# A fused attention, expert and feed-forward kernel: the attention loop goes by two head pairs at a time

## The chip, the core and the metric

The kernel runs on one core of one Trainium2 chip. TensorE (PE in the profile) multiplies matrices, VectorE (DVE) and ScalarE (ACT) work element by element, GpSimd (POOL) does indirect transfers and some fills, and SyncE (SP) issues the other transfers. Each engine takes its own instructions in the order in which they were written, and waits for other engines by semaphores. The metric is the time of one execution in microseconds.

## The reference

Three stages follow each other on 2304 tokens (4 sequences of 576) of width 512. Cut to what matters:

```python
# 1: attention, 8 heads of 64, causal window of 128, a slope per head
scores = q @ k.T / 8 - slope[h] * |i - j|;  masked where not 0 <= i - j < 128
attn = exp(scores - max);  attn = attn / (attn.sum(-1) + 1e-9)
x = attn @ v                                  # heads side by side: [2304, 512]
# 2: experts; tokens with x @ w_skip > 0 go to one of 8 experts
e = argmax(x @ w_gate);  gate = softmax(x @ w_gate)[e]
x[chosen] += gate * (relu(x @ w1[e]) @ w2[e])
# 3: feed-forward
h = x @ w_in;  out = (h * tanh(softplus(h))) @ w_out
```

All products are in float32. A float32 matmul shows as two passes in the trace, a transpose as one.

## The kernel before

Queries are taken in 18 tiles of 128 tokens, and each tile in four head pairs (`hp` 0 to 3), so the attention loop has 72 steps, one for each head pair of each tile. Keys lie in a ring of three tiles; a tile's scores need its own keys and those of the tile before, 256 columns. One head pair goes through these stages:

- **S**, `scores` (L357): two matmuls, one for each head, on the lower and the upper 64 rows of the array, each into a PSUM bank of its own (`qbanks`, three in rotation). DVE adds the bias table and takes the row's minimum of the negated scores (L373), ACT takes the exponential and its row sum into `pr` (L376).
- **F**, `flip` (L381): four 128 by 128 transposes of `pr` into a PSUM tile `pt` (two buffers, which the routing's `rp` and `idp` share); DVE copies it out to `ps` for head pair 0, and for head pair 2 of odd tiles, ACT for the others (L387 to L390).
- **V**, `values` (L394): for two blocks of keys, two matmuls side by side, each on 64 columns of the array, into `xu`; ACT copies two head pairs to `xs` together (L406).
- **T**, `turn_back` (L408): one matmul turns a head pair's values back to token rows, and computes its part of the routing logits, into `xw`, two PSUM banks.
- `finish` (L423): DVE multiplies two head pairs by the inverse row sums (L430, L433); `logits` (L440) adds the routing logits over heads (L445); `keep` and the gates' transfer write the rows to DRAM.

The order is written out by hand. Step `n` emits the scores of head pair `n`, the transposes of head pair `n - 2`, and then what was put down for that step in a table `later`: values after `VLAG` = 3 steps, turn-backs for two head pairs together after 5 or 6 (`TLAG`), `finish`, and for every group of tiles the routing:

```python
            at(n + VLAG, values, n // NP, n % NP)
            at(n + TLAG + 1 - n % 2, turn_back, n // NP, n % NP)
        if 2 <= n < NS + 2:
            flip((n - 2) // NP, (n - 2) % NP)
```

The routing of a group of up to three tiles is some twenty small pieces, mostly DVE instructions. They stand in a list (`Fill`), from which one is taken at each `vf.take`: between the two DVE reductions of a head pair, and between the stages of a step. Two pieces hold matmuls: `rank` (two into `rp`, L481 and L482) and `enter` (twelve small ones into `idp` for three tiles, L496). In the first tile, bias tables are made on DVE between the scores (L198), and warm-up matmuls stand behind them (L580).

In the same loop SP loads each tile's queries, keys and values one tile ahead, and the weights of the first two experts, a 512 KB chunk every three steps. Behind the loop come the last routing, a loop over experts with too many tokens (no round of it runs here), the gather of the first expert's tokens (L722), the eight experts (L743, L752) and the feed-forward part.

Of the kernel before, what the change touches and what calls it, by code (L numbers as in the profile page):

```python
# [27 lines left out]
P = 128  # L28
# [27 lines left out]
UNITS = (2,2,2,2,2,2,2,2)  # L56
WARMD = 32
WARME = 3
VLAG = 3
TLAG = 5  # L60
FILL = [[0,0],[0,1],[0,1],[0,1]]
GMAX = max(GROUPS)
GR = [(0, CAP // 2), (CAP // 2, CAP)]
# [40 lines left out]
def fused_kernel(ctx: ExitStack, tc: tile.TileContext, t):  # L104
# [246 lines left out]


    xu = pu.tile([P, NP, P], F32, name="xu")
    xw = pw.tile([P, 2, 512], F32, name="xw")
    qbanks = [pq.tile([P, 2, KW], F32, name=f"qs{x}")[:, 0, :] for x in range(3)]

    def scores(i, hp):  # L357
        d = tiles[i]
        qs = [qbanks[(8 * i + 2 * hp + hh) % 3] for hh in range(2)]
        q = qts[i]  # L360
        for hh in range(2):
            r = slice(hh * 64, hh * 64 + 64)
            if i == 0:
                ks, outs = [slice(0, 1)] * 2, [qs[hh][:, x * P:x * P + P] for x in range(2)]
            else:
                ks, outs = [slice(0, KR, KR - 1) if i % KR == 0 else slice(i % KR - 1, i % KR + 1)], [qs[hh]]
            for s, o in zip(ks, outs):
                nc.tensor.matmul(out=o, lhsT=q[r, hp, :], rhs=kring[r, hp, s, :], start=True, stop=True)  # L368
        sb = ap.tile([P, 2, KW], F32, name=f"sb{i}_{hp}", tag="sb")
        pr = ap.tile([P, 2, KW], F32, name=f"pr{i}_{hp}", tag="pr", bufs=3)  # L370
        for hh in range(2):
            h = 2 * hp + hh
            nc.vector.tensor_tensor_reduce(out=sb[:, hh, :], in0=qs[hh], in1=d['bt'][:, h, :], scale=-0.125,  # L373
                                           scalar=3.0e38, op0=ALU.add, op1=ALU.min, accum_out=d['mn'][:, h:h + 1])
            vf.take(FILL[hp][hh])
            nc.scalar.activation(out=pr[:, hh, :], in_=sb[:, hh, :], func=AF.Exp,  # L376
                                 bias=d['mn'][:, h:h + 1], scale=-1.0, accum_out=d['rs'][:, h:h + 1])
        d['pr', hp] = pr

    def flip(i, hp):  # L380
        d = tiles[i]  # L381
        pt = pp.tile([P, 512], F32, name=f"pt{i}_{hp}", tag="pt")
        prv = d['pr', hp].rearrange("p h k -> p (h k)")
        for k in range(4):
            nc.tensor.transpose(out=pt[:, k * P:k * P + P], in_=prv[:, k * P:k * P + P], identity=ident)
        ps = ap.tile([P, 512], F32, name=f"ps{i}_{hp}", tag="ps", bufs=3)
        if hp == 0 or hp == 2 and i % 2:  # L387
            nc.vector.tensor_copy(out=ps, in_=pt)
        else:
            nc.scalar.copy(out=ps, in_=pt)  # L390
        d['ps', hp] = ps

    def values(i, hp):
        d = tiles[i]  # L394
        if hp == 0:
            d['xs'] = ap.tile([P, NP, P], F32, name=f"xs{i}", tag="xs")
        ps = d['ps', hp]
        blocks = [0, 1] if i > 0 else [1]
        for x in blocks:
            y = 1 - x if i % KR == 0 else x  # L400
            for hh in range(2):
                h = 2 * hp + hh
                nc.tensor.matmul(out=xu[hh * 64:hh * 64 + 64, hp, :], lhsT=vts[i - 1 + x][:, h * 64:h * 64 + 64],
                                 rhs=ps[:, (2 * hh + y) * P:(2 * hh + y) * P + P], start=x == blocks[0], stop=x == 1)
        if hp % 2 == 1:
            nc.scalar.copy(out=d['xs'][:, hp - 1:hp + 1, :], in_=xu[:, hp - 1:hp + 1, :])  # L406

    def turn_back(i, hp):  # L408

        d = tiles[i]  # L410
        nc.tensor.matmul(out=xw[:, hp // 2, (hp % 2) * IW:(hp % 2 + 1) * IW], lhsT=d['xs'][:, hp, :], rhs=iw[:, hp, :],
                         start=True, stop=True)

    def sums(i):
# [7 lines left out]
    def finish(i, x):  # L422

        d = tiles[i]
        if x == 0:
            d['xt'] = ap.tile([P, XW], F32, name=f"x{i}", tag="x", bufs=GMAX + 2)
            d['lt'] = ap.tile([P, H, 9], F32, name=f"lt{i}", tag="lt")
        src = xw[:, x, 0:2 * IW].rearrange("p (a w) -> p a w", a=2)
        rr = d['rr'][:, 4 * x:4 * x + 4].rearrange("p (a b one) -> p a b one", a=2, one=1)
        nc.vector.tensor_tensor(out=d['xt'][:, x * KW:x * KW + KW].rearrange("p (a b d) -> p a b d", a=2, b=2),  # L430
                                in0=src[:, :, 0:P].rearrange("p a (b d) -> p a b d", b=2),
                                in1=rr.to_broadcast([P, 2, 2, 64]), op=ALU.mult)
        nc.vector.tensor_tensor(out=d['lt'][:, 4 * x:4 * x + 4, :].rearrange("p (a b) e -> p a b e", a=2),  # L433
                                in0=src[:, :, P:IW].rearrange("p a (b e) -> p a b e", b=2),
                                in1=rr.to_broadcast([P, 2, 2, 9]), op=ALU.mult)
# [100 lines left out]
    def routing(gi, i0, n, wait):  # L536
        choose, seat, enter = route(gi, i0)
        first(choose)
        for k, pieces in enumerate((seat, enter)):
            if wait:  # L540
                at(n + (k + 1) * wait, first, pieces)
            else:
                first(pieces)

# [9 lines left out]
            expert_chunk(k // 8, k % 8)  # L554

    for c in range(16):
        at(12 + 3 * c, expert_chunks, c)
    dec = [decode_pieces(n) for n in range(32)]

    ORDER = [*range(16), *range(16 + 2 * NDIR, 32), *range(16, 16 + 2 * NDIR)]  # L560
    for k in range(4):
        at(L1 + 2 * k, dec[ORDER[k]][0])

    NS = NT * NP
    n = 0
    while n < NS or any(k >= n for k in later):
        if n < NS:
            if n % NP == 0:
                i = n // NP
                load_until(i + 1)  # L570
                start_tile(i)
            if n in (2, 6, 10):
                vf.add(*bias_table(n // 4 + 3, ((6, 12, 15), (13,), (14,))[n // 4]))
            if n < NP:
                table0[n]()
            scores(n // NP, n % NP)
            if n < NP:
                table1[n]()
                for k in range(WARMS[n]):
                    nc.tensor.matmul(out=xw[:, 1, 0:256], lhsT=warm[:, 0:P], rhs=warm, start=True, stop=True)  # L580
            at(n + VLAG, values, n // NP, n % NP)
            at(n + TLAG + 1 - n % 2, turn_back, n // NP, n % NP)
            if n % NP == 1:
                at(n + TLAG, finish, n // NP, 0)
            if n % NP == NP - 1:
                i = n // NP
                gi, k, i0 = group_of[i]
                at(n + 1, sums, i)
                at(n + TLAG, finish, i, 1)
                at(n + TLAG, logits, i)  # L590
                at(n + TLAG + 1, keep, i)
                if k == GROUPS[gi] - 1:
                    at(n + TLAG + 1, routing, gi, i0, n + TLAG + 1, max(0, min(3, NT - 1 - i)))
        if 2 <= n < NS + 2:
            flip((n - 2) // NP, (n - 2) % NP)
        vf.take(0)
        for fn, args in later.get(n, []):
            fn(*args)
        vf.take(0)
        if n >= NS - 1:  # L600
            vf.take(0)
            vf.take(0)
        n += 1
    while vf.urgent:
        vf.take(0)
# [490 lines left out]
```

## Time and profile before

| | us |
|---|---|
| median of 3 runs (lowest, highest) | 782.83 (782.24, 784.47) |
| the profiled execution | 784.04 |
| its span | 782.2 |
| PE busy | 755.4 |
| DVE busy | 550.2 |
| ACT busy | 381.0 |
| scores of tile 2 begin, in the span | 20.90 |
| scores of the second half of tile 17 begin | 151.22 |
| the first expert's matmuls begin | 177.83 |

Busy times are of the whole span; times in rows count from the span's start. Timeline rows give the start, the duration from the first instruction's start to the last one's end, the engine, the line, the operation with its operands by the program's names, the shape of the array that a matmul uses (as 64\*128: rows by columns), the operands' sizes, and the number of instructions merged into the row. In brackets stands the idle time of the engine before it and what ended it. Durations of neighbouring matmuls overlap, so blocks are compared by their starts.

### The profile page before, as it was taken

Reading aid. Unit: us, or ns where it says so; the run is one execution under the profiler, and the core shown is the slowest. Engines: PE = TensorE matmul, PEld = TensorE weight load, DVE = VectorE, ACT = ScalarE, POOL = GpSimd, SP = SyncE. Lnnn points to the kernel's source line nnn. Section 1 sums busy time; section 2 is a strip of 40 time slices with the busy share of each in tenths; the row PEclk is TensorE's granted clock in tenths of the full one; section 3 lists DMA queues with packets and bytes.
Section 4 is the critical chain, followed back from the end, with each engine's and each line's share of the span. In section 5 each row is a group of like instructions: output and inputs, shape, how many; then the busy total and the mean of one; then the engine's idle time right before and its main releaser. Section 6 shows DMA issues by size and latency. Waiting matters only on the chain.

```text
span 782.2 us, 12363 instructions
## 1 busy us (share of the span) xinstructions
PE 755.4 (97%) x4489; PEld 627.1 (80%) x4489; DVE 550.2 (70%) x1419; ACT 381.0 (49%) x894; POOL 38.9 (5%) x57
## 2 busy tenths in 40 slices
PE   9999999959999999898999999999999999999997
PEld 6666666639999999897888787888888888888885
DVE  6887677745655546642788888777777778777776
ACT  5777777704443333322445454444544444444453
POOL 0100000010222111100000000000000000000000
PEclk9999999979999999999999999999999999999999
DMA  6576778424798999933112002000200002000100
GB/s 194 181 245 205 246 258 256 163 92 161 238 323 319 325 372 334 335 99 117 34 43 80 0 1 95 13 1 1 80 26 4 1 0 81 1 0 1 55 1 27
DMA packets 50767, 97.92 MB, mean 125 GB/s; under 512 B 5265, under 2 KB 15889, under 8 KB 50705
## 3 DMA queue, kind: packets, MB, share of 16 engines
q1 hardware_dynamic: 48656, 90.82, 34.3%
q0 software_dynamic: 2048, 6.30, 2.5%
q8 instruction: 36, 0.59, 0.3%
q14 instruction: 27, 0.21, 0.1%
HBM read 76.38 MB, written 20.72 MB: 124 GB/s over the span
## 4 chain that ended last, share of the span: by engine, by line
PE 47%; DVE 14%; DMA 6%; ACT 6%; issue 3%; SPq 1%; POOL 0%; POOLq 0%; DVEq 0%; another core or an unknown queue 0%; ACTq 0%
PE yd L986 15%; PE hq L743 7%; PE yp L752 7%; PE hd L924 5%; PE hd L922 5%; PE hd L923 5%; DMA wdo<-bits 4%; ACT r L942 3%; DVE r L950 2%; DVE nn L939 2%; ACT r L943 2%; DVE gl L965 2%; DVE uu L953 1%; DVE uu L947 1%; DVE ee L936 1%
## 5 line engine op out<-in xcount | busy, mean ns | idle before, releaser
L942 ACT ACTIVATE r<-nn,ln 128x512 f32<-128x512 f32 (+1 forms) x80 | 54.5, 682 | 153.7 <-DVE nn L939 153.7
L922 PE MATMUL hd<-xhl,wi 128*128 128x512 f32 (+1 forms) x320 | 119.3, 373 | 1.6 <-DVE gg L957 1.5
L924 PE MATMUL hd<-xhl,wi 128*128 128x512 f32 (+1 forms) x320 | 117.8, 368 | 0.0
L923 PE MATMUL hd<-xhl,wi 128*128 128x512 f32 (+1 forms) x320 | 117.8, 368 | 0.0
L986 PE MATMUL yd<-wo,gh 128*128 128x512 f32 x432 | 111.4, 393 | 1.6 <-ACT gh L961 1.6
L986 PEld LDWEIGHTS yd<-wo,gh 128*128 128x128 f32 x432 | 79.4, 188 | 17.8 <-ACT gh L961 2.5
L752 PE MATMUL yp<-hT,we 128*128 128x192 f32 x512 | 90.9, 327 | 1.6 <-ACT hT L744 1.6
L376 ACT ACTIVATE pr<-sb,mn 128x256 f32<-128x256 f32 x144 | 72.0, 500 | 41.7 <-DVE mn L373 38.2
L947 DVE TENSOR_TENSOR uu<-nn,r 128x512 f32<-128x512 f32 (+1 forms) x80 | 51.0, 637 | 51.8 <-ACT r L943 51.7
L743 PE MATMUL hq<-xTe,we 128*128 128x192 f32 x512 | 86.0, 326 | 1.0 <-ACT xTe L732 0.6
L752 PEld LDWEIGHTS yp<-hT,we 128*128 128x128 f32 x512 | 82.8, 190 | 2.0 <-ACT hT L744 1.9
L743 PEld LDWEIGHTS hq<-xTe,we 128*128 128x128 f32 x512 | 83.2, 190 | 1.5 <-ACT xTe L732 0.8
L373 DVE CUSTOM_DVE_ANT_0 sb<-qs,bias 128x256 f32<-128x256 f32 x144 | 56.8, 419 | 28.1 <-PE qs L368 26.2
L922 PEld LDWEIGHTS hd<-xhl,wi 128*128 128x128 f32 x320 | 60.2, 188 | 16.9 <-DVE gg L957 6.8
L924 PEld LDWEIGHTS hd<-xhl,wi 128*128 128x128 f32 x320 | 60.2, 188 | 10.1
L923 PEld LDWEIGHTS hd<-xhl,wi 128*128 128x128 f32 x320 | 60.2, 188 | 9.9
L986 PE MATMUL yd<-wo,gl 128*128 128x512 f32 x216 | 60.9, 389 | 0.0
L933 ACT ACTIVATE ee<-hd 128x512 f32<-128x512 f32 (+1 forms) x80 | 44.3, 553 | 33.7 <-PE hd L924 33.7
L965 DVE TENSOR_TENSOR gl<-gg,gh 128x512 fp32r<-128x512 f32 (+1 forms) x80 | 50.6, 633 | 9.4 <-ACT gh L961 9.3
L368 PE MATMUL qs<-kr,q 64*128 64x256 f32 (+1 forms) x304 | 51.6, 414 | 0.0
L957 DVE SCALAR_TENSOR_TENSOR gg<-uu,hd 128x512 f32<-128x512 f32 (+1 forms) x80 | 50.3, 629 | 0.6
L939 DVE SCALAR_TENSOR_TENSOR nn<-ee 128x512 f32<-128x512 f32 (+1 forms) x80 | 50.5, 632 | 0.1
(117 smaller groups left out, 1107.2 us busy)
## 6 DMA issues: line engine op xcount, KB each, us to landing
we<-w SPq DMA_DIRECT2D x64, 512.0 KB, 7.0
r<-w_in SPq DMA_DIRECT2D x16, 512.0 KB, 5.1
r<-w_out SPq DMA_DIRECT2D x16, 512.0 KB, 6.9
xd<-x SPq DMA_DIRECT2D x18, 256.5 KB, 3.9
v<-vv SPq DMA_DIRECT2D x18, 256.0 KB, 3.8
x<-x SPq DMA_DIRECT2D x18, 256.0 KB, 3.6
xt<-x SPq DMA_DIRECT2D x18, 256.0 KB, 3.0
out<-yo SPq DMA_DIRECT2D x18, 256.0 KB, 2.0
```

What stands on the lines that cost most here:

```text
L373: nc.vector.tensor_tensor_reduce(out=sb[:, hh, :], in0=qs[hh], in1=d['bt'][:, h, :], scale=-0.125, scalar=3.0e38, op0=ALU.add, op1=ALU.min ...
L376: nc.scalar.activation(out=pr[:, hh, :], in_=sb[:, hh, :], func=AF.Exp, bias=d['mn'][:, h:h + 1], scale=-1.0, accum_out=d['rs'][:, h:h + 1])
L743: nc.tensor.matmul(out=hq[:, 0:CAP], lhsT=w[:, c, fs], rhs=xT[:, c, :], start=c == 0, stop=c == NC - 1)
L752: nc.tensor.matmul(out=yp[:, 0:CAP], lhsT=w[:, f // 2, cs:cs + P], rhs=hT[:, f, :], start=f == 0, stop=f == 7)
L922: nc.tensor.matmul(out=hv, lhsT=wt[:, 0, fs], rhs=xhl[:, 0, c, 0:W], start=c == 0, stop=False)
L923: nc.tensor.matmul(out=hv, lhsT=wt[:, 0, fs], rhs=xhl[:, 1, c, 0:W], start=False, stop=False)
L924: nc.tensor.matmul(out=hv, lhsT=wt[:, 1, fs], rhs=xhl[:, 0, c, 0:W], start=False, stop=c == NC - 1)
L939: V.scalar_tensor_tensor(out=g['nn'], in0=g['ee'], scalar=2.0, in1=g['ee'], op0=ALU.add, op1=ALU.mult)
L942: A.activation(out=g['r0'], in_=g['nn'], func=AF.Ln, bias=ln2, scale=1.0)
L947: V.tensor_tensor(out=g['uu'], in0=g['nn'], in1=g['r0'], op=ALU.mult)
L965: V.tensor_tensor(out=g['gl'], in0=g['gg'], in1=g['gh'].bitcast(F32), op=ALU.subtract)
L986: nc.tensor.matmul(out=yds[bi][k], lhsT=g[:, k * P:k * P + P], rhs=wt[:, h, ws], start=f == 0 and x == 0, stop=f == 15 and x == 2)
```

## The change

The loop goes by supersteps of two head pairs, half a tile. Superstep `n` emits the scores of both its head pairs, then the transposes of both pairs of superstep `n - 1` (`FLAG`), the turn-backs of `n - 3` (`TLAG`), the values of `n - 2` (`VLAG`) with ACT's copy of them, and then what stands in `later`. The scores have four banks instead of three, each used once in a superstep; `xw` goes from two banks to one; `pr` and `ps` get a fourth buffer. Steps put down for the experts' weights and the routing are halved, and the routing's second and third part follow two supersteps apart instead of three steps.

```diff
-VLAG = 3
-TLAG = 5
+FLAG = 1
+VLAG = 2
+TLAG = 3
...
-    xw = pw.tile([P, 2, 512], F32, name="xw")
-    qbanks = [pq.tile([P, 2, KW], F32, name=f"qs{x}")[:, 0, :] for x in range(3)]
+    xw = pw.tile([P, 512], F32, name="xw")
+    qbanks = [pq.tile([P, 2, KW], F32, name=f"qs{x}")[:, 0, :] for x in range(4)]
...
-        qs = [qbanks[(8 * i + 2 * hp + hh) % 3] for hh in range(2)]
+        qs = [qbanks[2 * (hp % 2) + hh] for hh in range(2)]
...
-        pr = ap.tile([P, 2, KW], F32, name=f"pr{i}_{hp}", tag="pr", bufs=3)
+        pr = ap.tile([P, 2, KW], F32, name=f"pr{i}_{hp}", tag="pr", bufs=4)
...
-        if hp % 2 == 1:
-            nc.scalar.copy(out=d['xs'][:, hp - 1:hp + 1, :], in_=xu[:, hp - 1:hp + 1, :])
+
+    def take_values(i, x):
+        nc.scalar.copy(out=tiles[i]['xs'][:, 2 * x:2 * x + 2, :], in_=xu[:, 2 * x:2 * x + 2, :])
...
-                at(n + (k + 1) * wait, first, pieces)
+                at(n + (1 + k * (wait > 1)) * wait, first, pieces)
...
-    NS = NT * NP
+    NS = 2 * NT
+    pairs = lambda m: [(m // 2, m % 2 * 2 + x) for x in range(2)]
...
-            scores(n // NP, n % NP)
...
-            at(n + VLAG, values, n // NP, n % NP)
-            at(n + TLAG + 1 - n % 2, turn_back, n // NP, n % NP)
...
+            for _, hp in pairs(n):
+                if i == 0:
+                    table0[hp]()
+                scores(i, hp)
...
+            at(n + TLAG, finish, i, half)
...
-                    at(n + TLAG + 1, routing, gi, i0, n + TLAG + 1, max(0, min(3, NT - 1 - i)))
-        if 2 <= n < NS + 2:
-            flip((n - 2) // NP, (n - 2) % NP)
+                    at(n + TLAG, routing, gi, i0, n + TLAG, max(0, min(2, NT - 1 - i)))
+        vf.take(0)
+        if FLAG <= n < NS + FLAG:
+            for p in pairs(n - FLAG):
+                flip(*p)
+        vf.take(0)
+        if TLAG <= n < NS + TLAG:
+            for p in pairs(n - TLAG):
+                turn_back(*p)
+        if VLAG <= n < NS + VLAG:
+            for p in pairs(n - VLAG):
+                values(*p)
+            take_values((n - VLAG) // 2, (n - VLAG) % 2)
         vf.take(0)
         for fn, args in later.get(n, []):
             fn(*args)
```

How the instructions stand is shown for PE at two places. The first is a stretch without routing, in tile 4; the names carry the tile and the head pair (`pt4_0`: tile 4, head pair 0), `qs0` to `qs3` are the score banks. Before:

```order
L368 MATMUL qs0_177<-kr_120,q4_485 128x256
L368 MATMUL qs1_178<-kr_120,q4_485 128x256
L385 MATMUL pt4_0_680<-ident_128,pr4_0_611 128x128 x4
L411 MATMUL xw_176<-iw_140,xs3_596 128x146 x2
L403 MATMUL xu_175<-ps3_3_653,v2_275 64x128 x2
L403 MATMUL xu_175<-ps3_3_653,v3_373 64x128 x2
L368 MATMUL qs2_179<-kr_120,q4_485 128x256
L368 MATMUL qs0_177<-kr_120,q4_485 128x256
L385 MATMUL pt4_1_711<-ident_128,pr4_1_639 128x128 x4
L403 MATMUL xu_175<-ps4_0_685,v3_373 64x128 x2
L403 MATMUL xu_175<-ps4_0_685,v4_488 64x128 x2
```

Now, one superstep:

```order
L369 MATMUL qs0_177<-kr_120,q5_597 128x256
L369 MATMUL qs1_178<-kr_120,q5_597 128x256
L369 MATMUL qs2_179<-kr_120,q5_597 128x256
L369 MATMUL qs3_180<-kr_120,q5_597 128x256
L386 MATMUL pt4_2_751<-ident_128,pr4_2_668 128x128 x4
L386 MATMUL pt4_3_758<-ident_128,pr4_3_679 128x128 x4
L413 MATMUL xw_176<-iw_140,xs3_640 128x146 x2
L404 MATMUL xu_175<-ps4_0_692,v3_369 64x128 x2
L404 MATMUL xu_175<-ps4_0_692,v4_484 64x128 x2
L404 MATMUL xu_175<-ps4_1_699,v3_369 64x128 x2
L404 MATMUL xu_175<-ps4_1_699,v4_484 64x128 x2
```

The same matmuls stand in four blocks instead of seven. The second place is the `rank` piece of the first group, on PE. Before, between the scores and the transposes:

```order
L368 MATMUL qs0_177<-kr_120,q5_601 128x256
L368 MATMUL qs1_178<-kr_120,q5_601 128x256
L481 LDWEIGHTS trib_156
L481 MATMUL rp0_775<-ohall_165,trib_156 128x24
L482 LDWEIGHTS ones_158
L482 MATMUL rp0_775<-cum0_167,ones_158 128x24
L385 MATMUL pt4_3_782<-ident_128,pr4_3_704 128x128 x4
```

Now:

```order
L369 MATMUL qs0_177<-kr_120,q5_597 128x256
L369 MATMUL qs1_178<-kr_120,q5_597 128x256
L483 LDWEIGHTS trib_156
L483 MATMUL rp0_791<-ohall_165,trib_156 128x24
L484 LDWEIGHTS ones_158
L484 MATMUL rp0_791<-cum0_167,ones_158 128x24
L369 MATMUL qs2_179<-kr_120,q5_597 128x256
L369 MATMUL qs3_180<-kr_120,q5_597 128x256
L386 MATMUL pt5_0_815<-ident_128,pr5_0_730 128x128 x4
```

The piece has moved in between the two score pairs of a superstep; the twelve `idp` matmuls of `enter`, which stood between values and scores, now stand there too.

## Rows read from the trace of the kernel before

**Rows 1.** The page: busy time by engine, and granted clock by slice in tenths

```profile
PE 755.4 (97%) x4489; PEld 627.1 (80%) x4489; DVE 550.2 (70%) x1419; ACT 381.0 (49%) x894; POOL 38.9 (5%) x57
...
PEclk9999999979999999999999999999999999999999
```

**Rows 2.** Busy time by stretch: stretch, length, each engine's busy time, clock, DMA

```profile
40.00:60.00 20.00, 20.00 (x184) 13.73 (x181) 15.51 (x84) 14.24 (x49) 0.40 (x2) 1.00 0.81 251
60.00:80.00 20.00, 20.00 (x188) 13.71 (x188) 15.16 (x80) 15.14 (x52) 0.00 (x0) 1.00 0.69 199
100.00:120.00 20.00, 20.00 (x186) 13.88 (x186) 14.09 (x70) 14.98 (x50) 0.00 (x0) 1.00 0.80 257
```

**Rows 3.** PE's timeline, one cycle of two head pairs: start, duration, operation

```profile
62.75 0.70 PE L368 MATMUL qs<-kr,q 64*128 64x256 f32 x4
63.38 0.66 PE L385 MATMUL pt<-ident,pr 128*128 128x128 f32 x4
63.87 0.66 PE L411 MATMUL xw<-iw,xs 128*128 128x146 f32 x4
64.47 0.66 PE L403 MATMUL xu<-ps,v 128*64 128x128 f32 x8
65.06 0.70 PE L368 MATMUL qs<-kr,q 64*128 64x256 f32 x4
65.69 0.65 PE L385 MATMUL pt<-ident,pr 128*128 128x128 f32 x4
66.27 0.66 PE L403 MATMUL xu<-ps,v 128*64 128x128 f32 x8
66.86 0.49 PE L368 MATMUL qs<-kr,q 64*128 64x256 f32 x2
```

**Rows 4.** PE's timeline, short windows: blocks without their first matmuls

```profile
63.07 0.38 PE L368 MATMUL qs<-kr,q 64*128 64x256 f32 x2
...
63.55 0.49 PE L385 MATMUL pt<-ident,pr 128*128 128x128 f32 x3
...
64.63 0.50 PE L403 MATMUL xu<-ps,v 128*64 128x128 f32 x6
...
64.85 0.28 PE L403 MATMUL xu<-ps,v 128*64 128x128 f32 x2
```

**Rows 5.** PE's timeline around `rank` (rp) and `enter` (idp)

```profile
149.38 0.70 PE L368 MATMUL qs<-kr,q 64*128 64x256 f32 x4
...
150.07 0.63 PE L385 MATMUL pt<-ident,pr 128*128 128x128 f32 x4
...
79.25 0.70 PE L496 MATMUL idp<-num,pl 128*96 128x8 bf16 x12
79.88 0.70 PE L368 MATMUL qs<-kr,q 64*128 64x256 f32 x4
```

**Rows 6.** Timeline of PE and DVE: ends of the steady stretch, last normalization

```profile
20.90 0.70 PE L368 MATMUL qs<-kr,q 64*128 64x256 f32 x4
...
151.22 0.70 PE L368 MATMUL qs<-kr,q 64*128 64x256 f32 x4
...
161.82 0.42 DVE L430 TENSOR_TENSOR x<-xw,rr 128x256 f32<-128x256 f32 x1 [0.42 <-PE xw L411]
```

**Rows 7.** Timeline of DVE and of ACT in the cycle of rows 3

```profile
63.59 0.42 DVE L373 CUSTOM_DVE_ANT_0 sb<-qs,bias 128x256 f32<-128x256 f32 x1 [1.03 <-PE qs L368]
...
63.94 0.42 DVE L373 CUSTOM_DVE_ANT_0 sb<-qs,bias 128x256 f32<-128x256 f32 x1
...
64.58 0.42 DVE L430 TENSOR_TENSOR x<-xw,rr 128x256 f32<-128x256 f32 x1 [0.21 <-PE xw L411]
...
64.06 0.51 ACT L376 ACTIVATE pr<-sb,mn 128x256 f32<-128x256 f32 x1 [0.24 <-DVE mn L373]
...
64.56 0.49 ACT L376 ACTIVATE pr<-sb,mn 128x256 f32<-128x256 f32 x1
```

**Rows 8.** SyncE's waits from 20 to 160, and transfers with time to landing

```profile
SPq L153 <- PE pt L385: 50.5, 15, 4.3
...
kr<-kT SPq DMA_DIRECT2D x11, 256.0 KB, 3.7
```

More of the change, by code (lines that the diff above doesn't have):

```diff
@@ L385, in flip @@
             nc.tensor.transpose(out=pt[:, k * P:k * P + P], in_=prv[:, k * P:k * P + P], identity=ident)
-        ps = ap.tile([P, 512], F32, name=f"ps{i}_{hp}", tag="ps", bufs=3)
+        ps = ap.tile([P, 512], F32, name=f"ps{i}_{hp}", tag="ps", bufs=4)
         if hp == 0 or hp == 2 and i % 2:
@@ L404, in values @@
                                  rhs=ps[:, (2 * hh + y) * P:(2 * hh + y) * P + P], start=x == blocks[0], stop=x == 1)
-        if hp % 2 == 1:
-            nc.scalar.copy(out=d['xs'][:, hp - 1:hp + 1, :], in_=xu[:, hp - 1:hp + 1, :])
+    def take_values(i, x):
+        nc.scalar.copy(out=tiles[i]['xs'][:, 2 * x:2 * x + 2, :], in_=xu[:, 2 * x:2 * x + 2, :])
     def turn_back(i, hp):
         d = tiles[i]
-        nc.tensor.matmul(out=xw[:, hp // 2, (hp % 2) * IW:(hp % 2 + 1) * IW], lhsT=d['xs'][:, hp, :], rhs=iw[:, hp, :],
+        nc.tensor.matmul(out=xw[:, (hp % 2) * IW:(hp % 2 + 1) * IW], lhsT=d['xs'][:, hp, :], rhs=iw[:, hp, :],
                          start=True, stop=True)
@@ L556, in fused_kernel @@
     for c in range(16):
-        at(12 + 3 * c, expert_chunks, c)
+        at((12 + 3 * c) // 2, expert_chunks, c)
     dec = [decode_pieces(n) for n in range(32)]
@@ L561, in fused_kernel @@
     for k in range(4):
-        at(L1 + 2 * k, dec[ORDER[k]][0])
-    NS = NT * NP
+        at(L1 // 2 + k, dec[ORDER[k]][0])
+    NS = 2 * NT
+    pairs = lambda m: [(m // 2, m % 2 * 2 + x) for x in range(2)]
     n = 0
@@ L567, in fused_kernel @@
         if n < NS:
-            if n % NP == 0:
-                i = n // NP
+            i, half = n // 2, n % 2
+            if half == 0:
                 load_until(i + 1)
                 start_tile(i)
[L572 to L575, printed above, removed]
-            scores(n // NP, n % NP)
[L577 to L580, printed above, removed]
-            at(n + VLAG, values, n // NP, n % NP)
-            at(n + TLAG + 1 - n % 2, turn_back, n // NP, n % NP)
[L583 to L586, printed above, removed]
+            if n in (1, 3, 5):
+                vf.add(*bias_table(n // 2 + 3, ((6, 12, 15), (13,), (14,))[n // 2]))
+            for _, hp in pairs(n):
+                if i == 0:
+                    table0[hp]()
+                scores(i, hp)
+                if i == 0:
+                    table1[hp]()
+                    for k in range(WARMS[hp]):
+                        nc.tensor.matmul(out=xw[:, 0:256], lhsT=warm[:, 0:P], rhs=warm, start=True, stop=True)
+            at(n + TLAG, finish, i, half)
+            if half:
                 gi, k, i0 = group_of[i]
                 at(n + 1, sums, i)
-                at(n + TLAG, finish, i, 1)
                 at(n + TLAG, logits, i)
-                at(n + TLAG + 1, keep, i)
+                at(n + TLAG, keep, i)
                 if k == GROUPS[gi] - 1:
-                    at(n + TLAG + 1, routing, gi, i0, n + TLAG + 1, max(0, min(3, NT - 1 - i)))
-        if 2 <= n < NS + 2:
-            flip((n - 2) // NP, (n - 2) % NP)
+                    at(n + TLAG, routing, gi, i0, n + TLAG, max(0, min(2, NT - 1 - i)))
[11 more added lines that the diff above has]
+            take_values((n - VLAG) // 2, (n - VLAG) % 2)
         vf.take(0)
@@ L600, in fused_kernel @@
         if n >= NS - 1:
-            vf.take(0)
-            vf.take(0)
+            for _ in range(4):
+                vf.take(0)
         n += 1
```

2 lines of the change are left out of this document (1 added, 1 removed).

## The prediction

> **What bounds the kernel now.** I read the page first. The whole program is bound by TensorE: 97% of the span busy, at the full granted clock except in slice 9 [rows 1]. The change touches the attention loop alone, so I asked for busy time by stretch there: PE is busy for 20.00 of 20.00 us in the stretches of the loop, DVE for 14 to 16 and ACT for 14 to 15, granted clock 1.00 [rows 2]. An engine without a gap says only that instructions stand close together, not that each is short. So I went on to PE's timeline of one clean cycle, two head pairs without routing work [rows 3]. Its blocks begin at 62.75 (scores, S), 63.38 (transposes, F), 63.87 (turn-back, T), 64.47 (values, V), 65.06 (S), 65.69 (F), 66.27 (V) and again 66.86: 4.11 us. The reader is to look at the column of operand shapes: S runs on 64 rows by 128 columns, F and T on 128 by 128, V on 128 by 64. The shape of the array changes six times in a cycle (S to F, T to V, V to S, S to F, F to V, V to S).
>
> What a change of shape costs is read inside the blocks, where later instructions of a block are shown apart [rows 4]. In F the second transpose starts 0.17 us after the first (63.55 against 63.38), but the next three steps, the last of them into T, take 63.55 to 63.87, 0.107 each: going from F to T, with other operands but the same shape, costs nothing. In V the second pair of matmuls starts 0.16 after the first (64.63), the next two steps take 0.11 each (64.85), and the last pair needs 0.21 until S begins (65.06): entry and exit pay 0.05 and 0.10 over the pitch of 0.11. In S the second pass starts 0.32 after the first (63.07 against 62.75), and F follows 0.31 later.
>
> **The change, part by part.**
>
> *One superstep against two steps.* No matmul is added or removed; a superstep holds the same 8 passes of S (four pairs side by side), 8 transposes, 4 turn-back passes and 16 value passes (8 pairs) as the cycle above, in four blocks with three changes of shape instead of six. S with four pairs: 0.32 + 2 x 0.21 + 0.31 = 1.06. The pitch of 0.21 inside is not in the trace of before, where a block has only two passes: below it is bounded by the columns (256 against 128 at 0.107, so 0.21), above by the first step of 0.32. I take 0.21, since the row nearest to it, F's inner steps, runs at the columns' rate. F: 0.17 + 7 x 0.107 = 0.92. T: 0.60, as in [rows 3]. V: 0.16 + 6 x 0.11 + 0.21 = 1.03. Sum 3.61 against 4.11: 0.50 less for each superstep; with the upper bound for S 3.82.
>
> *The steady stretch.* The scores of tile 2 begin at 20.90 and those of the second half of tile 17 at 151.22 [rows 6]: 130.3 us, 31 supersteps. Check: 31 x 4.11 = 127.4, and the order puts four idp blocks and five rp blocks between. An idp block adds 0.63 (79.25 to 79.88) and an rp block 0.06 (S to F in 0.69 instead of 0.63) [rows 5]: 127.4 + 2.5 + 0.3 = 130.2. After: 31 x 3.61 = 111.9. Now rp and idp stand between the two score pairs of one superstep, so each splits the S block and pays for leaving S (0.31 - 0.21 = 0.10) and for entering it again (0.32 - 0.21 = 0.11): idp 0.63 + 0.10 + 0.11 = 0.84, and rp, which stood beside F in its own shape, 0.06 + 0.10 + 0.10 + 0.11 = 0.37. Four of each: 4.8. Sum 116.7; the stretch gives back 13.6 us.
>
> *Start.* Up to 20.90 the bias tables on DVE hold the first scores back, and their number is the same. The supersteps 2 and 3 lie in it; merged blocks may give 0 (DVE sets it) to 1.7 us. I take 1.0.
>
> *End.* From the scores at 151.22 to the last tile's second normalization at 161.82 pass 10.6 us [rows 6]. After: the last full superstep with rp 3.61 + 0.37 = 3.98, then F 0.92, T 0.60, V 1.03 (6.5), idp 0.63, T (7.8; its operand is copied by ACT meanwhile), V (8.8), the copy with its hand-over about 0.6, T 0.6 and 0.25 until DVE starts: 10.3. Between 1 us shorter and 1 us longer; I take 0. Routing, gather and all behind it stay as they are.
>
> *What hides the rest.* The lag from scores to transposes falls from two steps (4.11 us) to one superstep, and four score banks, all used in each superstep, replace three in rotation. DVE starts its first reduction 0.84 after S begins (63.59) and the next 0.35 later (63.94) [rows 7]; four end at 0.84 + 4 x 0.35 + 0.07 = 2.3, and S returns to the banks at 3.61: 1.3 to spare. ACT starts the first exponential 0.47 after DVE (64.06) and repeats every 0.50 (64.56): the fourth ends at 3.3, and the transposes that want it begin at 3.61 + 1.06 = 4.67: 1.4 to spare. Routing pieces between the reductions use some of this, not all. Over a cycle DVE is busy 15.16/20 x 4.11 = 3.1 us and ACT 14.98/20 x 4.11 = 3.1 [rows 2]; both fit into 3.61, at 86%. For queues that pile up in the supersteps with routing I add 0.7 us in all (0 to 3).
>
> *Loads.* SyncE's wait for the previous tile's scores before a key load is the longest of its own [rows 8]. A tile's keys land 3.7 us after issue; they may be issued when the last scores of the tile before are done and are wanted three supersteps less one S later, 3 x 3.61 - 1.06 = 9.8 us. That stays hidden. The transfers' busy share of 0.81 [rows 2] becomes 0.81 x 4.11/3.61 = 0.92, still below full.
>
> **Sum.** 13.6 + 1.0 + 0 - 0.7 = 13.9. The profiled execution took 784.04 (span 782.2 and 1.8 around it), so 770.1; the median of the three timed runs is 782.83, 1.2 lower, so the forecast is 769.0, with 766 to 772 as its own range.
>
> **Rivals.**
>
> *DVE or ACT becomes the bound.* For it: 86% of a superstep busy, a strict order on each, and the tiles whose transposes ACT copies out twice in one superstep. The superstep would settle between 3.7 and 3.95: 31 x 0.1 to 0.34 of the gain is lost, 3 to 10 us, so 772 to 779. Against it: DVE idles 1.03 us in front of the first reduction of the cycle and 0.21 in front of the normalization, both times for PE [rows 7]. The Trainium skill, "TensorEngine Tiling (Array Packing)", section "PSUM Bottleneck", warns that when TensorE speeds up, the copies out of PSUM may be what remains; here the rows leave 14% for it.
>
> *The cost belongs to each group, not to the change of shape.* Then merging groups would pay it again inside, and the time stays at 781 to 785. Against it: F to T in 0.10 without a gap, with a new operand on both sides [rows 3, 4].
>
> *The clock falls (slower).* Place: the loop, where eight transposes now stand together. At the lower of the two levels, 1.2 GHz, the streamed part of a superstep (S 4 x 0.21, F 8 x 0.107, T 4 x 0.125 and V 8 x 0.11, about 3.1 us) doubles, so from about 5 of the 31 supersteps at that level on the gain is gone; with a third of the loop there the time would be 769 + 10 x 3.1 = 800. Against it: transposes make a part of every cycle now, and the granted clock stands at 1.00 throughout [rows 2]; slice 9, the only one in the middle of the span with less, is where PE runs out of work behind the loop [rows 1]. The Trainium skill, "TensorE: Matmul & The Clock Gate", section "Part 4: PE-mode transpose", states that transposes do not count as PE activity in the way that matmuls do; by that rule longer runs of them would speak for this rival, and the trace does not bear it out so far.
>
> *More than forecast.* A faster start (1.7) and end (1.0) and no pile-up: 766 and a little below.
>
> **How the numbers follow.** Forecast 0.64, DVE or ACT bound 0.18, no cost of shape 0.05, clock 0.03, more than forecast 0.10. The range from 765.5 to 776 holds the forecast, most of the first rival and a part of the last. A measurement of this kernel tells about 0.3% (2.3 us) from no change. Faster: the forecast, the first rival, the last, 0.92. Same: most of the group rival, 0.04. Slower: the clock, 0.03, and 0.01 of the group rival with a longer end.
>
> **What would show it.** PE's timeline: blocks of S, F, T and V at 1.06, 0.92, 0.60 and 1.03, a clean superstep at 3.61, S after V and F after S at the steps shown above; S(tile 2) to S(tile 17, second half) in about 117 us; rp and idp inside the S block. The first rival would show as idle PE in front of F or S with an ACT or DVE releaser; the second as steps of 0.3 inside the S block and 0.16 inside F and V; the clock as less than 1.00 between 20 and 140 us. The prediction is wrong if the clean superstep is above 3.8, or if what the loop gains is lost between its end and the first expert.

## The result, and the profile after

The changed kernel takes 765.57 us (median of 4 runs, 764.50 to 767.14) against 783.57 for the kernel before (4 runs, 782.24 to 784.47): ratio 0.9773, 95% interval 0.9748 to 0.9798. That is 18.0 us less; 13.9 were forecast, the time lies 3.4 us below the forecast of 769.0 and 0.1 us inside the lower edge of the range (765.5). The profiled execution took 766.14 (span 764.3).

Read it in the order in which the kernel before was read. The page of the changed kernel, busy time by engine and the granted clock by slice, against [rows 1]:

```profile
PE 740.0 (97%) x4489; PEld 632.2 (83%) x4489; DVE 548.5 (72%) x1419; ACT 378.4 (50%) x894; POOL 39.1 (5%) x57
...
PEclk9999999889999999999999999999999999999999
```

The counts are the same to the instruction, and TensorE is still busy 97% of a shorter span. Nothing was taken out; the same matmuls stand closer. Busy time by stretch (columns as in [rows 2]):

```profile
40.00:60.00 20.00, 20.00 (x209) 15.87 (x210) 15.95 (x84) 16.02 (x57) 0.00 (x0) 1.00 0.94 278
60.00:80.00 20.00, 20.00 (x206) 15.71 (x204) 16.07 (x85) 16.48 (x56) 0.00 (x0) 1.00 0.93 278
100.00:120.00 20.00, 20.00 (x198) 16.06 (x199) 16.20 (x86) 15.98 (x56) 0.00 (x0) 1.00 0.86 254
```

PE has no gap, as before, but 198 to 209 matmuls in 20 us instead of 184 to 188. DVE and ACT rise to 80 to 82% busy, the transfers' share to 0.86 to 0.94, the clock stays at 1.00. PE's timeline shows a clean superstep from 63.92 on, then one with rp and one with idp (against [rows 3] and [rows 5]):

```profile
63.92 1.13 PE L369 MATMUL qs<-kr,q 64*128 64x256 f32 x8
64.98 1.09 PE L386 MATMUL pt<-ident,pr 128*128 128x128 f32 x8
65.91 0.66 PE L413 MATMUL xw<-iw,xs 128*128 128x146 f32 x4
66.51 1.09 PE L404 MATMUL xu<-ps,v 128*64 128x128 f32 x16
67.53 0.70 PE L369 MATMUL qs<-kr,q 64*128 64x256 f32 x4
68.16 0.19 PE L483 MATMUL rp<-ohall,trib 128*128 128x24 bf16 x1
68.20 0.17 PE L484 MATMUL rp<-cum,ones 128*128 128x24 bf16 x1
68.31 0.70 PE L369 MATMUL qs<-kr,q 64*128 64x256 f32 x4
68.94 1.10 PE L386 MATMUL pt<-ident,pr 128*128 128x128 f32 x8
...
75.10 0.70 PE L369 MATMUL qs<-kr,q 64*128 64x256 f32 x4
75.74 0.70 PE L498 MATMUL idp<-num,pl 128*96 128x8 bf16 x12
76.37 0.49 PE L369 MATMUL qs<-kr,q 64*128 64x256 f32 x2
```

From start to start: S 1.06, F 0.93, T 0.60, V 1.02, together 3.61. With rp, S takes 67.53 to 68.94, 1.41 instead of 1.06, so rp costs 0.35; an idp block adds its own 0.63 and again 0.20 for splitting S, 0.83 in all. The ends of the loop and the last normalization, PE and DVE, against [rows 6]:

```profile
19.38 0.49 PE L369 MATMUL qs<-kr,q 64*128 64x256 f32 x2
...
136.11 0.70 PE L369 MATMUL qs<-kr,q 64*128 64x256 f32 x4
...
146.23 0.42 DVE L432 TENSOR_TENSOR x<-xw,rr 128x256 f32<-128x256 f32 x1
```

136.11 - 19.38 = 116.7 us, against 130.3. I call this stretch "the loop" below: from the scores of tile 2 to those of the second half of tile 17. DVE and ACT at the scores of the superstep above, against [rows 7]:

```profile
64.76 0.42 DVE L374 CUSTOM_DVE_ANT_0 sb<-qs,bias 128x256 f32<-128x256 f32 x1 [0.31 <-PE qs L369]
...
65.23 0.51 ACT L377 ACTIVATE pr<-sb,mn 128x256 f32<-128x256 f32 x1 [0.66 <-DVE mn L374]
```

DVE waits 0.31 us for PE and ACT 0.66 for DVE, even with routing pieces between: neither holds PE up. PE's blocks say the same: all 23 unsplit S blocks of the loop take 1.06 from start to start, all 31 of V 1.02. The loads, SyncE's wait for PE and a key load's time to landing, against [rows 8]:

```profile
SPq L154 <- PE pt L386: 11.4, 13, 1.7
...
kr<-kT SPq DMA_DIRECT2D x14, 256.0 KB, 5.3
```

Keys land later after their issue, 5.3 us instead of 3.7, but SyncE waits less before it issues them (11.4 instead of 50.5), and PE waits for no load in the loop.

By stages, each from the two traces: first scores 0.8 us earlier (5.5 against 6.3 after the span's start; the profiles of the other kernels below, with the same work up to there, show 5.1 to 6.3, so this belongs to single executions); from there to the loop 0.75 less; loop 13.6 less; loop's end to the last x 0.5 less (10.1 against 10.6); from there to the first expert matmul 0.7 less; experts 0.6 more; last stage 2.2 less (406.1 against 408.3, from its first matmul to the start of its last). The sum is 17.9, the difference of the spans.

### The profile page after: what moved, and what is told of

It reads as the page before. It is cut to its first block, busy times and chain, and to the rows that moved or that the text cites. A ratio compares the mean times of both kernels' runs of the same rounds, so it can differ in the third digit from the quotient of the medians.

```text
span 764.3 us, 12404 instructions
## 1 busy us (share of the span) xinstructions
PE 740.0 (97%) x4489; PEld 632.2 (83%) x4489; DVE 548.5 (72%) x1419; ACT 378.4 (50%) x894; POOL 39.1 (5%) x57
## 4 chain that ended last, share of the span: by engine, by line
PE 57%; DVE 11%; ACT 5%; DMA 4%; issue 2%; POOL 0%; POOLq 0%; SPq 0%; DVEq 0%; another core or an unknown queue 0%; ACTq 0%
PE yd L996 19%; PE yp L762 9%; PE hq L753 8%; PE hd L932 6%; PE hd L934 6%; PE hd L933 6%; DMA wdo<-bits 2%; ACT r L952 2%; DVE r L960 2%; DVE nn L949 2%; ACT r L953 1%; DVE gl L975 1%; DVE uu L957 1%; DMA xt<-x 1%; DVE uu L963 1%
## 5 line engine op out<-in xcount | busy, mean ns | idle before, releaser
L933 PE MATMUL hd<-xhl,wi 128*128 128x512 f32 (+1 forms) x320 | 117.8, 368 | 0.0
L933 PEld LDWEIGHTS hd<-xhl,wi 128*128 128x128 f32 x320 | 60.3, 188 | 10.1
L934 PEld LDWEIGHTS hd<-xhl,wi 128*128 128x128 f32 x320 | 60.3, 188 | 10.1
L960 DVE SCALAR_TENSOR_TENSOR r<-r,uu 128x512 f32<-128x512 f32 (+1 forms) x80 | 50.5, 631 | 0.1
```

What stands on the lines that cost most here:

```text
L933: nc.tensor.matmul(out=hv, lhsT=wt[:, 0, fs], rhs=xhl[:, 1, c, 0:W], start=False, stop=False)
L934: nc.tensor.matmul(out=hv, lhsT=wt[:, 1, fs], rhs=xhl[:, 0, c, 0:W], start=False, stop=c == NC - 1)
L960: V.scalar_tensor_tensor(out=g['r0'], in0=g['r0'], scalar=2.0, in1=g['uu'], op0=ALU.mult, op1=ALU.add)
```

## The experiments

All of these ran beside the kernel before on the same chip, on several chips in turn; the ratio is to that, and ratios are what is compared between experiments. "Loop" is the stretch defined above, in the profiled execution (before 130.3, changed kernel 116.7). The texts of what was expected call the transposes "turns" at times; "turn-backs" are T. The edits are shortened.

### Undo the order, keep the buffers: order_back

The changed kernel's buffers and lags, but one head pair at a time:

```diff
-            for _, hp in pairs(n): scores(i, hp)
-        ... flip(*p), turn_back(*p), values(*p) for both pairs
+        for x in range(2):
+            scores(i, pairs(n)[x][1])
+            flip(*pairs(n - FLAG)[x])
+            if x == 0: both turn-backs of n - TLAG
+            values(*pairs(n - VLAG)[x])
```

> The changed kernel with its buffers, banks and lags, but PE's blocks put back in the order of before inside each superstep: scores and transposes of the first pair, turn-backs, values of the first pair, then scores, transposes and values of the second. If the changes of the array's shape are the cost, a clean superstep takes 4.11 us again instead of 3.61 (six changes, not three), and the time is 779 to 782. If the gain came from the fourth score bank, the deeper buffers or the other lags, the time stays near 766.

Measured: 792.52 us, ratio 1.0118 (1.0091 to 1.0145), loop 140.5. A miss: 10 us slower than either theory had it. PE's timeline and then ACT's, in a clean half of a superstep:

```profile
66.67 0.66 PE L386 MATMUL pt<-ident,pr 128*128 128x128 f32 x4
67.43 0.77 PE L413 MATMUL xw<-iw,xs 128*128 128x146 f32 x4
68.12 0.66 PE L404 MATMUL xu<-ps,v 128*64 128x128 f32 x8
...
67.01 0.36 ACT L408 COPY xs<-xu 128x256 f32<-128x256 f32 x1
```

F to T takes 0.76 (0.49 in [rows 3]) and T 0.69 instead of 0.60. T multiplies `xs`, which ACT copies until 67.37; T starts at 67.43. That is 0.36 a superstep, 31 times, 11 us, about what this loop is longer than that of the kernel before (10.2): a wait that my edit made by putting the turn-backs too early. The steps from 68.12 on, V and S and F, are those of the kernel before (next S at 68.71, F at 69.34).

### The same with the turn-backs later: order_back_late

```diff
-            if x == 0 and TLAG <= n < NS + TLAG:
+            if x == 1 and TLAG <= n < NS + TLAG:
```

> The buffers and lags of the changed kernel, TensorE's blocks again one head pair at a time, but with both turn-backs in the second half of a superstep (scores, turn, values, scores, turn, turn-backs, values), where ScalarE's copy of the value products has had time. Theory A (the time follows the count of shape changes, and what order_back lost beyond that was TensorE's wait for this copy): clean superstep 4.11 us as in the kernel before, 31 supersteps 0.50 longer than in the changed kernel, 766 + 15 = 779 to 782. Theory B (order_back lost it to something in the buffers that it shares with the changed kernel): 788 to 793 again.

Measured: 784.11 us (10 runs, 780.03 to 787.45), ratio 1.0001 (0.9984 to 1.0018), loop 129.9. The wait is gone, the blocks of [rows 3] are back at the same durations (4.12 from one T to the next), and so is the time of the kernel before. Its profiled execution, 780.03, the fastest of the ten, lies in the expected range and the median 2 us above it; I have no cause for that difference beside the scatter of the runs. Against the changed kernel the only difference is the order of the blocks, and with it the places of the routing's pieces. It is worth 13.2 us in the loop and, by the ratios 1.0001 and 0.9773, 18 us of the whole.

### The buffers alone: buffers_alone

```diff
-    xw = pw.tile([P, 2, 512], F32, name="xw")
-    qbanks = [... for x in range(3)]
+    xw = pw.tile([P, 512], F32, name="xw")
+    qbanks = [... for x in range(4)]
... pr and ps bufs=3 -> bufs=4, all else as before
```

> The kernel before with the new buffers alone: four score banks by parity, one bank for the turn-backs, four buffers for pr and ps; order and lags as before. Shape theory: a clean cycle of 4.11 us and 782 to 785, no difference from before. If banks or buffers had held PE back, part of the 18 us would show here: below 780.

Measured: 784.33 us, ratio 1.0001 (0.9984 to 1.0018), loop 130.3, the same as before to 0.01 us. Four score banks and the fourth buffers do nothing by themselves, and the one `xw` bank costs nothing.

### Part of the batching: scores_apart

Scores and transposes by one pair, turn-backs and values by two. A superstep is S F S F T V, with five changes of shape (S to F, F to S, S to F, T to V, V to S), where the kernel before has six and the changed kernel three.

```diff
-            for _, hp in pairs(n): scores(i, hp)
-        ... flip(*p) for both pairs
+        for x in range(2):
+            scores(i, pairs(n)[x][1])
+            flip(*pairs(n - FLAG)[x])
         turn_back(*p) and values(*p) for both pairs, as in the changed kernel
```

> The changed kernel with scores and transposes by one pair (S F S F T V V), values and turn-backs batched as changed: five changes of shape in a superstep. By the steps read in the blocks, the second S to F costs 0.16 and F to S 0.20 more: a clean superstep of 3.97 us, and about 775 us in all (773 to 777). If only batching the values mattered, the superstep would stay at 3.6 and the time at 766; if only batching the scores and transposes, 4.1 and 780.

Measured: 775.01 us, ratio 0.9889 (0.9862 to 0.9917), loop 125.3. PE's timeline, one superstep:

```profile
60.60 0.70 PE L369 MATMUL qs<-kr,q 64*128 64x256 f32 x4
61.23 0.66 PE L386 MATMUL pt<-ident,pr 128*128 128x128 f32 x4
61.73 0.66 PE L413 MATMUL xw<-iw,xs 128*128 128x146 f32 x4
62.32 1.09 PE L404 MATMUL xu<-ps,v 128*64 128x128 f32 x16
63.34 0.70 PE L369 MATMUL qs<-kr,q 64*128 64x256 f32 x4
63.98 0.66 PE L386 MATMUL pt<-ident,pr 128*128 128x128 f32 x4
64.56 0.70 PE L369 MATMUL qs<-kr,q 64*128 64x256 f32 x4
```

60.60 to 64.56 is 3.96, against 4.11 with six changes and 3.61 with three: the joined values, which save one change, are worth 0.15, and the joined scores and transposes, which save the other two, 0.35.

### Where the routing's pieces stand: three other places

In the changed kernel rp and idp come between the two score pairs. They draw their PSUM buffer from the same two as the transposes. The edit lets `Fill.take` pass over them at some places:

```diff
-    def take(self, n=1):
-        if self.urgent:
+    def take(self, n=1, inside=False):
+        if self.urgent and not (inside and self.urgent[0].__name__ in ('rank', 'enter')):
```

routing_outside: not between the scores, so just before the transposes.

> The changed kernel with the two routing pieces that hold matmuls kept out of the score block: rp and idp now come between scores and transposes. Shape theory: rp costs 0.06 instead of 0.35 and idp 0.63 instead of 0.83, five and four times: 2 to 2.5 us less than the changed kernel, 763 to 764. If DVE's waits for these pieces set the time there, no difference or a loss.

Measured: 767.36, ratio 0.9801 (0.9776 to 0.9826), loop 117.8. A miss. PE's timeline:

```profile
45.95 0.19 PE L483 MATMUL rp<-ohall,trib 128*128 128x24 bf16 x1
...
46.01 0.64 PE L386 MATMUL pt<-ident,pr 128*128 128x128 f32 x4
47.25 0.66 PE L386 MATMUL pt<-ident,pr 128*128 128x128 f32 x4 [0.60 <-DVE ps L487]
```

rp itself takes only 0.06, but the second pair of transposes wants the buffer that rp still holds until DVE has read it at L487, behind three score reductions. T starts at 47.74; with F's 0.93 it would have started 0.86 earlier without rp.

routing_behind_turns: not before the transposes, so just behind them.

> The changed kernel, with the routing's two pieces of TensorE work (rp, the ranks, and idp, the entries) kept out of the score block and out of the place just before the turns: they can now come only behind the turns of a superstep, so the next turns find their buffers free again. Theory A (a piece costs 0.06 us of its own and a change of shape, and what routing_outside lost was the turns' wait for the buffer that rp had taken): rp costs 0.1 to 0.2 in place of 0.34, idp 0.65 in place of 0.83, some 1.5 us less in the loop, 763.5 to 765. Theory B (a piece costs the loop the same wherever it stands, since it sets VectorE's work back): 765 to 767.

Measured: 773.95, ratio 0.9888 (0.9866 to 0.9910), loop 122.7. Both theories fall: by the ratios 9 us slower than the changed kernel. The same buffer, on its other side:

```profile
46.10 1.09 PE L386 MATMUL pt<-ident,pr 128*128 128x128 f32 x8
48.03 0.17 PE L483 MATMUL rp<-ohall,trib 128*128 128x24 bf16 x1 [0.84 <-DVE ps L389]
...
48.08 0.75 PE L413 MATMUL xw<-iw,xs 128*128 128x146 f32 x4
```

Now rp waits until a copy has taken the transposes out, 0.8 us of idle time for each piece, and PE does nothing meanwhile, since the rest stands behind it: F to T takes 1.98 instead of 0.93, and T then 0.68 instead of 0.60.

routing_behind_values: only behind the values, before the next scores.

> The changed kernel with rp and idp kept out of every place but the one behind the value products, just before the next superstep's scores. There the turns' two buffers have been free for over a microsecond, and rp's buffer has the whole score block (1.07 us) to be read before the next turns want it. Theory A (what the two runs before lost was the shared pair of buffers, on one side or the other; the piece itself costs little): no idle TensorE in the loop, rp 0.1 to 0.25 in place of 0.34, idp 0.6 to 0.7 in place of 0.83, the loop 115 to 116 in place of 116.7, 764 to 765.5. Theory B (a piece costs its place in the order whatever the place): 766 or more.

Measured: 763.91 us (5 runs, 763.46 to 767.70), ratio 0.9769 (0.9745 to 0.9793), loop 115.1. PE's timeline:

```profile
47.20 1.09 PE L404 MATMUL xu<-ps,v 128*64 128x128 f32 x16
48.23 0.19 PE L483 MATMUL rp<-ohall,trib 128*128 128x24 bf16 x1
48.37 1.14 PE L369 MATMUL qs<-kr,q 64*128 64x256 f32 x8
```

No wait on either side, rp costs 0.14 instead of 0.35, and the loop is 1.6 us shorter, as theory A had it (the time lies 0.1 below its range). The gain is read from the trace; in the runs it is too small to be told apart from the changed kernel's 0.9773.

### Fewer changes still: four_changes, four_early, four_mid

A whole tile at a time: S of four pairs, F of two, T of two, V of four, F of two, T of two. That makes four changes of shape a tile (S to F, T to V, V to F, T to S), two fewer than two supersteps of the changed kernel have; the text below says four fewer, but its 6.87 is reckoned with two. The other transposes have to wait since there are two buffers for them.

```diff
+            for hp in range(NP):
+                scores_mm(i, hp)
...
+        flip(n - 1, 0); flip(n - 1, 1); turn_back(n - 3, 0); turn_back(n - 3, 1)
+        for hp in range(NP): values(n - 2, hp)
+        flip(n - 1, 2); flip(n - 1, 3); turn_back(n - 3, 2); turn_back(n - 3, 3)
```

> A whole tile at a time, so four shape changes fewer to a tile than two supersteps have: scores of all four head pairs, turns of two, their turn-backs, values of four, turns of two, turn-backs of two. Theory A (each shape change costs about 0.15 to 0.2 us, DVE and ACT do not bind yet): clean tile 6.87 us against 2 x 3.61 = 7.22, about 15 tiles, 760 to 762. Theory B (DVE and ACT, busy 80 to 84 of 100 in the changed kernel's loop, bind now: scores of four pairs in a row need all eight score halves free, and TensorE waits there for DVE): clean tile 7.2 or more, 766 to 772.

Measured: 782.47 us, ratio 0.9991 (0.9970 to 1.0012), loop 120.7. This kernel leaves the counts of the two tiles before out of the last tile's ranks, so its output is not the reference's; what is read from it is where PE waits in the loop, which comes before that. A clean tile takes 6.87 as forecast, but few are clean. PE's waits in the loop (in all, times, longest):

```profile
PE qs L371 <- DMA kr<-kT: 6.7, 5, 2.1
PE idp L504 <- DVE ps L395: 2.9, 4, 0.7
PE rp L489 <- ACT ps L397: 2.4, 2, 1.2
```

Neither theory: the scores of a whole tile want its keys earlier than before, and they had not landed.

four_early: the loads moved up, and the counts put into the last tile's ranks again.

```diff
-            load_until(i + 1)
...
+            if i + 2 < NT: load_tile(i + 2)      # behind the scores
+            if i + 2 < NT: load_values(i + 2)    # behind the values
```

> four_changes with the loads mended: queries and keys of the tile after next are loaded as soon as the scores of a tile are done, its values behind the value products, where four_changes began a tile's loads only one tile ahead; the last tile's ranks are also made after the counts of the two tiles before it, which four_changes left out for that tile. Theory A (TensorE's idle time of some 11 us in the loop of four_changes was the wait for those loads): clean tile 6.87 all along, the loop about 110 to 112 in place of 120.7; the longer drain of the three tiles in flight stays (some 14 us from the last scores to the last x, against 10.1 from the last scores in the changed kernel), together 768 to 771. Theory B (DVE and ACT are the bound at four changes): TensorE still idles 0.3 to 0.7 us a tile, 774 or more.

Measured: 771.98 us, ratio 0.9860 (0.9831 to 0.9889), loop 113.9. The wait for keys is gone; what is left of the three lines is the routing's (idp 3.0, rp 2.4), the one that the runs above had made out. The time missed its range by 1 us: the loop is 2 us above it, and the drain of three tiles, from the loop's end to the last x, 20.6 us, where I had 14.

four_mid: rp and idp in the middle of the scores, as in the changed kernel.

> four_early with rp and idp only in the middle of the score block, where both buffers of the turns are free. Theory A (the 0.74 of idle time before each idp and the up to 1.19 before each rp were the wait for these buffers, and nothing else holds four changes back): no idle TensorE in the loop, which is 107 to 109.5 in place of 113.9; with the drain of three whole tiles as in four_early 765 to 768, beside the changed kernel. Theory B (DVE or ACT bind once that wait is gone): idle time of TensorE turns up at the scores or turns, loop 111 or more, 769 to 772.

Measured: 767.59 us, ratio 0.9797 (0.9780 to 0.9815), loop 108.6. Loop and time as theory A had them, if not quite without idle time: PE idles 1.0 us in all in the loop, at two idp (0.8) and two rp, and six of the 15 steps from tile to tile take the 6.87 or 6.88 of a clean one, so DVE and ACT don't bind there. The loop is 8.1 us shorter than the changed kernel's, and 11.1 are lost in the drain (21.3 against 10.1), where each tile goes through its steps with nothing else to fill them:

```profile
134.15 1.14 PE L392 MATMUL pt<-ident,pr 128*128 128x128 f32 x8 [0.76 <-ACT ps L397]
...
140.41 0.17 PE L490 MATMUL rp<-cum,ones 128*128 128x24 bf16 x1 [1.19 <-DVE cum L485]
```

### The last stage: before_out4 and after_out4

The last stage is not touched by the change, but is 2.2 us shorter in the profile. Its output tiles have two buffers, and wait for the store of the one two before. Both kernels with one ring of four:

```diff
-        xts[i] = dp.tile([P, DM], F32, name=f"xt_{i}", tag="xt")
+        xts[i] = dp.tile([P, DM], F32, name=f"xt_{i}", tag="xy", bufs=4)
-        yo = dp.tile([P, DM], F32, name=f"yo{i}", tag="yo")
+        yo = dp.tile([P, DM], F32, name=f"yo{i}", tag="xy", bufs=4)
```

> The kernel before, with one ring of four buffers for the last stage's input tiles and output tiles in place of two of each, so that an output tile does not wait for the store of the one two before it. Theory A (2 us of the gain beyond my sum came from a wait for such a store at a block boundary, which the changed kernel happens not to meet): 1.0 to 2.2 us faster than the kernel before, 781.4 to 782.5, and the last stage 406.2 in place of 408.3. Theory B (that wait is hidden or belongs to single executions): within 0.5 us of the kernel before.

> The same ring of four in the changed kernel. Theory A (the changed kernel does not meet the wait for the output store): within 0.4 us of the changed kernel, 765.2 to 766.5, so that the gain of the change alone would be 15.5 to 16.5 instead of 18. Theory B (the wait is in both kernels): 764 to 765, as much faster as before_out4 is over the kernel before.

Measured: before_out4 782.57 us (12 runs), ratio 0.9979 (0.9965 to 0.9994); after_out4 766.66 (5 runs), ratio 0.9772 (0.9749 to 0.9795), the same as the changed kernel's. Both times lie 0.1 to 0.2 us above theory A's ranges. Idle time before the copies into these tiles, by releaser (us, times), in the kernel before:

```profile
  DMA out<-yo: 8.4, 5
```

PE's timeline of the same kernel, in the last block:

```profile
740.72 0.39 PE L922 MATMUL hd<-xhl,wi 128*128 128x256 f32 x1 [1.19 <-DVE gg L957]
```

In before_out4 that idle time of PE is 0.3. The idle time before the copies in the changed kernel:

```profile
  DMA out<-yo: 3.9, 4
```

In before_out4 and after_out4 the line is gone, and their last stages take 405.5 both. The changed kernel meets this wait too, so its last stage gets 0.6 shorter, which its runs don't show; the kernel before, with 2.8 less, meets it at a worse moment (one of its copies on ACT waits 2.3 us). So theory A holds in its main point: about 1.6 us (0.5 to 2.7) of the 18 is this wait. Why its stores land later there was not tried.

## Why the prediction was right, and where its sum fell short

*One superstep.* Right to 0.01 us: 3.61, with S 1.06 (1.06 forecast), F 0.93 (0.92), T 0.60 (0.60), V 1.02 (1.03). The value chosen for S's pitch, between the bounds 0.21 and 0.32, was the lower, and that was the one. The experiments give it as a line: S takes 0.63, 1.06 and 1.93 for 4, 8 and 16 matmuls, V 0.59, 1.02 and 1.90 for 8, 16 and 32 (the longest in four_mid, S from 67.07 to 69.00 and V from 55.57 to 57.47). That is 0.108 for each matmul of S plus 0.20 for the block, and 0.055 for each of V plus 0.15. An F block that stands between two changes pays 0.15 as well: 0.58 before V in [rows 3], of which the pitch of 0.107 makes 0.43. The change saves one block of each: 0.20 + 0.15 + 0.15 is the 0.50. The constant is paid once for a block however long, and F to T shows none: this excludes the rival in which each group pays. (The forecast's terms for S, as printed, add up to 1.05; with the pitch at 0.214 they are 1.06.)

What the prediction didn't use is in the timeline of the weight loads (PEld), each of which brings a matmul's stationary operand in. The same superstep in the changed kernel:

```profile
64.98 0.86 PEld L386 LDWEIGHTS pt<-ident,pr 128*128 128x128 f32 x8 [0.33 <-issue]
65.80 0.55 PEld L413 LDWEIGHTS xw<-iw,xs 128*128 128x128 f32 x4
66.50 0.85 PEld L404 LDWEIGHTS xu<-ps,v 128*64 128x64 f32 x16
67.53 0.19 PEld L369 LDWEIGHTS qs<-kr,q 64*128 64x128 f32 x2 [0.17 <-DVE x L432]
```

From F to T, where the shape stays, T's first load begins 0.11 us before T (65.80 against 65.91). At the three changes of shape no load begins ahead: those of F, V and S begin with their blocks (64.98, 66.50, 67.53). In all a change costs the 0.15 to 0.20 us above. The Trainium skill, "TensorEngine Tiling (Array Packing)", section "Key Properties", says that a change of tiling mode drains TensorE; the trace agrees in that no load of the new shape runs ahead of its block. Whether the late load is the whole of that cost is not shown, and no run gave the blocks one shape in the old order: that the shape is the cause, and not a change of operands, rests on F to T, on rp in front of F (0.06, against 0.35 inside S), and on a cost that followed the number of changes in each order tried.

*The loop.* Right: 13.6 forecast, 13.6 measured, with four rp at 0.35 (0.37) and four idp at 0.83 (0.84). scores_apart, order_back_late and the four-change kernels, all with the same arithmetic, came out at their forecast per cycle.

*DVE or ACT as the bound.* Didn't happen, and four_mid shows by how much: at 6.87 instead of 7.22 for a clean tile they still don't hold PE up. The 0.7 us for queues that pile up was a term too much: PE doesn't idle once in the loop.

*The clock.* 1.00 in the loop, with eight transposes together. What the Trainium skill, "TensorE: Matmul & The Clock Gate", section "Part 4: PE-mode transpose", states of transposes and PE activity did not lower it here.

*Start and end.* 1.0 and 0 were forecast, though the count for the end gave 10.3 against 10.6 before. Measured: 0.75 up to the loop beside the 0.8 of the earlier first scores, 0.5 from the loop to the last x, and 0.7 from there to the first expert matmul, which I had put down as unchanged: behind the last x fewer routing pieces are left (8 idp matmuls instead of 12).

*The step that failed.* "Routing, gather and all behind it stay as they are." The 4 us beyond the sum are the 0.7 of pile-up, 0.5 more at the start, 1.2 between the loop and the first expert, and 2.2 in the last stage less 0.6 in the experts. The largest of them is the store, in a stage that the change doesn't touch and that I hadn't read; its row (8.4 us of idle before the copies) was in the trace of before. The change itself is worth about 16 us: 782.57 - 766.66 = 15.9 with the ring of four in both, by the two intervals give or take 2.

*Luck.* The mechanism and the loop's 13.6 us were right on their merits. That the time still lies in the range, by 0.1 us, is luck: the 4 us that the sum lacked used up the whole room below. The rival "More than forecast" came near at "766 and a little below": no pile-up, a start of 1.7 and an end of 1.0, where the trace shows none, 1.55 (with the 0.8 of the first scores, which belong to single executions) and 1.2. The store was in neither.

## What to carry to other kernels

Where PE has no gap, look at the operand shapes in its timeline: blocks of the same shape that stand apart for no reason of data each pay a constant (here 0.15 to 0.20 us), and the gain of joining them is the number of changes saved times this, until a buffer or a lag stops it. When such work is moved, look for whoever shares its buffers: at four places the same piece of routing (rp) cost TensorE 0.14, 0.35, about 0.85 and about 1.1 us. And a view without idle time doesn't show that an engine waits for nothing, as the next section says. A deeper batch is paid in the drain: the tile-wide version won 8 us in the loop and lost 11 behind it.

## What the runs showed of the hardware that was not expected

A wait in front of T cost more than the wait itself. T's stationary operand is the copy that it waits for, so its weight loads wait as well. The weight loads' timeline in order_back:

```profile
67.43 0.55 PEld L413 LDWEIGHTS xw<-iw,xs 128*128 128x128 f32 x4 [0.33 <-ACT xs L408]
```

They start together with T (67.43) and T takes 0.69. In order_back_late they start at 60.10, 0.11 before T (60.21), and T takes 0.60. The list of PE's waits names little of what order_back loses there, 0.5 us of some 11 in the loop (in all, times, longest):

```profile
PE xw L413 <- ACT xs L408: 0.5, 2, 0.3
```

Matmuls overlap in the trace, so a wait of 0.27 us between F and T leaves hardly a gap on PE. It is read from the starts of the blocks and from the weight loads.

The changed kernel's profiled execution has a stretch among the experts at the lower clock level, 1.2 GHz, which that of the kernel before has not:

```profile
311.90:315.20 3.30, 3.30 (x13) 3.17 (x12) 2.51 (x5) 1.31 (x3) 1.12 (x1) 0.50 0.87 251
```

The granted clock is the 0.50 behind the engines' busy times. Just before it PE had been idle for 2.03 us, waiting for ACT until 311.25:

```profile
311.25 2.38 PE L762 MATMUL yp<-hT,we 128*128 128x192 f32 x8 [2.03 <-ACT hT L754]
```

The steps of these matmuls grow from 0.16 to 0.32 us, and until 315.36 some 1.7 us are lost to it. The stretch falls among the experts, which take 0.6 us longer than before. It doesn't belong to the change: buffers_alone, in the order of before, has one among the experts too (clock 0.50 from 357.1 to 360.3), and routing_behind_values has none.
